# Attention, MoE and RMS-norm MoE in one kernel: low-weight transfers and half of the first v go to ScalarE's DMA queue, and the opening order changes

## The chip, the core and the metric

The kernel runs on one core of one Trainium2 chip. The metric is the device time of one execution in microseconds, as the median of several runs. TensorE does the matrix multiplications, VectorE, ScalarE and GpSimd the elementwise work, and SyncE issues DMA transfers. ScalarE can issue DMAs too, in its own instruction stream: such an instruction waits there for the buffer or the data that it needs, and what stands behind it on ScalarE waits with it.

## The reference

Three stages follow one another on 4608 tokens of width 512.

```python
def _attn_ref(q, k, v):          # (8, 8, 576, 64), in chunks of 64 tokens
    scores = scale * np.matmul(q_c, k_c.transpose(0, 1, 2, 4, 3))
    attn = np.exp(scores - np.max(scores, axis=-1, keepdims=True))
    attn = attn / (np.sum(attn, axis=-1, keepdims=True) + 1e-09)
    return np.matmul(attn, v_c)

def _moe_ref(x, w_gate, w_val, w_out):   # 512 -> 1536 -> 512
    g = x @ w_gate
    return (g * (1.0 / (1.0 + np.exp(-g))) * (x @ w_val)) @ w_out

def _moe2_ref(x, w_gate, w_val, w_out, rms_g):
    xn = x / np.sqrt(np.mean(x * x, axis=-1, keepdims=True) + 1e-06) * rms_g
    # then the same as _moe_ref, on xn
```

The result of the attention, laid out by tokens, is the x of the first MoE, and its result the x of the second. The weights arrive as 64-bit floating point numbers; q, k and v as 32-bit ones.

## The kernel before, in words

**Precision.** Each operand of a large product is kept as a high part, rounded to TensorE's fast 32-bit format, and a low part, the rest. A product is then three matmuls, high by high, high by low and low by high (mm3, lines 476 to 479).

**First MoE.** The tokens are cut into 9 blocks of 512 (index j), the hidden width into 12 tiles of 128 (index f). One iteration (j, f), of 108 in all, does emit_g (12 matmuls, then a tanh on ScalarE and a product on VectorE, line 490), emit_v (12 matmuls, then a product on VectorE, line 506, and a rounding of the hidden tile on ScalarE, line 509), and emit_y of the iteration before (12 matmuls into four PSUM banks that collect over f). The gate and the value have one PSUM bank each, so the next gate tile waits for line 490, the next value tile for line 506.

**Weights.** There are 36 weight tiles: g, v and o for each f. In block 0, the "head", they are loaded raw (pre_w1, line 979, through load_w64, line 101) and converted one by one. `conv1(z)` (line 995) works on tile z: `rebase` of tile z+1 (two passes on ScalarE, lines 112 and 116, the tiles cr and cm), `to_f32` of tile z (two passes on VectorE, lines 131 and 134, of which the second reads the first's result, and a rounding on ScalarE to the high part, line 144), `to_lo` of tile z-1 (a subtraction on VectorE, line 152, to the low part), and the next raw load. High parts stay in SBUF. Low parts do not fit: each is written to a scratch in DRAM (lo1_d, called lo_scratch in the trace) and read again in each of the blocks 1 to 8. Three buffers each hold low g and low v tiles, four low o tiles. In the head a new low tile needs a buffer whose write has landed and whose matmuls are done.

The writes are kept in a list, `keep`, and issued on SyncE when more than five are waiting (line 1006). `load_lo` (line 157) fetches the three low tiles of an iteration two iterations ahead, on SyncE as well, 96 times three loads; the first is called in the head, at f = 10.

**Attention.** It runs in tiles of 128 tokens. For the first four tiles it stands ahead of the first MoE and is written out by hand (lines 1026 to 1060): trans_tok transposes q and k on TensorE and copies them on ScalarE; att_s makes the scores; att_m subtracts the maximum (VectorE) and takes the exponential (ScalarE); att_n sums and inverts (VectorE) and scales (GpSimd); att_t transposes the probabilities on TensorE and copies them on ScalarE (line 408); att_pv multiplies by v and rounds to the high x (ScalarE, line 453); att_lo subtracts for the low x (VectorE, line 471). The later tiles are laid into the positions of the iterations, three to an iteration, by `put` and `spread`; `run(p)` calls what stands at a position. `spread` issues a list of loads on SyncE in equal parts over a number of positions.

**Order.** Every engine works through its own instructions in the order in which the program writes them. SyncE has nearly all DMAs: q and k of tiles 0 to 3 (load_tok, two each), v of the first eight chunks (load_v(0), 16 pieces of 64 KB) with the first raw weights between, later loads of q, k and v, the raw weights, the writes of low weights and the loads of them.

**After the first MoE.** The second MoE uses combinations of weight blocks and other loops (from line 1134); its weights come through load_ring on SyncE. The change does not touch it.

Of the kernel before, what the change touches and what calls it, by code (L numbers as in the profile page):

```python
# [9 lines left out]
F32 = mybir.dt.float32  # L10
# [9 lines left out]
def tile_kernel(  # L20
# [17 lines left out]
    nc = tc.nc  # L38
# [66 lines left out]
    keep = []  # L105
# [3 lines left out]
    def rebase(l, nm, f):  # L109
        high = stage[l, nm, f][:, :, 1]  # L110
        r = cv.tile([P, KD * P], U32, tag="cr", bufs=3, name=f"cr{nm}{f}_{l}")
        nc.scalar.activation(r.bitcast(F32), high.bitcast(F32), AF.Copy, scale=2.0 ** -112)
        m = None
        if l == 0:
            m = cv.tile([P, KD * P], U32, tag="cm", bufs=2, name=f"cm{nm}{f}_{l}")
            nc.scalar.activation(
                m, stage[l, nm, f][:, :, 0], AF.Copy,
                scale=2.0 ** -29 * (1.0 - 2.0 ** -16), bias=7.5 * 2.0 ** -16 - 0.5,
            )
        half[l, nm, f] = (r, m)  # L120

    def to_f32(l, nm, f):
        t = stage.pop((l, nm, f))
        low, high = t[:, :, 0], t[:, :, 1]
        r, m = half.pop((l, nm, f))
        if m is None:
            m = cv.tile([P, KD * P], U32, tag="cm", bufs=1, name=f"cm{nm}{f}_{l}")
            nc.vector.tensor_scalar(
                out=m, in0=low, scalar1=29, scalar2=None, op0=ALU.logical_shift_right
            )  # L130
        nc.vector.scalar_tensor_tensor(
            out=m, in0=high, scalar=0x80000000, in1=m, op0=ALU.bitwise_and, op1=ALU.bitwise_or
        )
        nc.vector.scalar_tensor_tensor(
            out=r, in0=r, scalar=3, in1=m, op0=ALU.logical_shift_left, op1=ALU.bitwise_or
        )
        r = r.bitcast(F32)
        if l == 0:
            hi = wraw.tile([P, KD * P], F32R, tag=f"w{nm}{f}", name=f"w{nm}{f}_0")
            whi[0, nm, f] = hi  # L140
        else:
            flat[nm, f] = r
            return
        nc.scalar.copy(hi, r)
        made[l, nm, f] = (r, hi)
# [11 lines left out]
    def load_lo(l, j, f):  # L157
        for z, nm in enumerate("gvo"):
            t = wlo.tile([P, KD * P], F32R, tag=f"l{nm}", bufs=LB[nm], name=f"l{nm}_{l}_{j}_{f}")
            nc.sync.dma_start(out=t.bitcast(F32), in_=lo1_d[z, f])  # L160
            wl_[l, j, f, nm] = t

    flat = {}
# [145 lines left out]
    def issue(dmas):  # L309
        for o, i in dmas:  # L310
            nc.sync.dma_start(out=o, in_=i)  # L311
# [332 lines left out]
    for x, (l, j) in enumerate(seq):  # L644
# [32 lines left out]
        if x > 0 and seq[x - 1][0] == 0:  # L677
# [8 lines left out]
            for d in range(KD):  # L686
                put(l, j, 28 + 2 * d, lambda pj=pj, d=d: rms_x(pj, d))

    w2 = [(nm, f) for fp in range(NP2) for nm in "gvo" for f in (fp, fp + NP2)]
    slots = [(j, 3 * f) for j in range(1, NB - 1) for f in range(0, NF, 2)]  # L690
    for (nm, f), (j, pos) in zip(w2, slots):
# [280 lines left out]
    with tc.manual_schedule():  # L972
# [22 lines left out]
        def conv1(z):  # L995
            if z < 0 or z > len(w1) + 2:
                return
            if z + 1 < len(w1):
                rebase(0, *w1[z + 1])
            if z < len(w1):  # L1000
                to_f32(0, *w1[z])
            if 0 < z <= len(w1):
                if z > 1:
                    to_lo(*w1[z - 1])
                pre_w1(z + 6 if z < 6 else 12 if z < 8 else z + 5)
            while len(keep) > (5 if z < len(w1) else 0):
                nc.sync.dma_start(out=keep[0][0], in_=keep[0][1])
                keep.pop(0)

        NI = NW // P  # L1010
# [2 lines left out]
        issue(load_tok(2))  # L1013
        issue(load_tok(3))
        first_v = load_v(0)
        issue(first_v[:len(first_v) // 2])
        pre_w1(1)
        issue(first_v[len(first_v) // 2:])
        pre_w1(3)
        issue(load_tok(4))  # L1020
        pre_w1(7)
        nc.sync.dma_start(out=rg, in_=moe2_rms_g.rearrange("(c p) -> p c", p=P))
        later = load_v(1)
        sb_ = ("a", "yb")
        xb_ = (("g", "v"), ("y0", "y1"))
        trans_tok(0, xb_[0])
        trans_tok(1, xb_[1])
        att_s(0, sb_[0])
        att_m(0)
        trans_tok(2, xb_[0])  # L1030
        att_s(1, sb_[1])
        att_m(1)
        trans_tok(3, xb_[1])
        att_n(0)
        att_s(2, sb_[0])
        att_m(2)
        att_n(1)
        att_s(3, sb_[1])
        rebase(0, *w1[0])
        att_m(3)  # L1040
        att_n(2)
        att_t(0, xb_[0][0])
        att_t(1, xb_[1][0])
        to_f32(0, *w1[0])
        att_n(3)
        att_pv(0, 0, "a")
        att_pv(1, 0, "yb")
        att_lo(0, 0)
# [3 lines left out]
        att_lo(1, 0)  # L1052
        att_pv(2, 0, "a")
        att_pv(3, 0, "yb")
        att_lo(2, 0)
        att_lo(3, 0)
        rebase(0, *w1[1])
        conv1(1)
        conv1(2)
        conv1(3)  # L1060
# [6 lines left out]
        for n, (l, j, f) in enumerate(iters):  # L1067
            def run(p):
                for fn in at.get(3 * n + p, ()):
                    fn()  # L1070

            head = (l, j) == (0, 0)
            if (j, f) == (1, 0):
                conv.close()
                cv = open_pool(conv, "cv2", 2, "right")
            if (j, f) == (NB - 1, 0):
                conv.close()
                attn.close()
                X2 = open_pool(two, "x2", 1, "right")
                x_load(0, 0)  # L1080
                xops = x_prep(0, 0)
            if (j, f) == (NB - 1, 8):
                load_ring(4)

            if head and f == 0:
                issue(later + load_tok(5))
            if head and f in (1, 2):
                issue(load_tok(5 + f))
                if f == 1:
                    issue(load_v(2))  # L1090
            if n + 2 < len(iters) and n + 2 >= NF:
                load_lo(*iters[n + 2])
            if (j, f) == (NB - 1, 8):
                x_load(0, 1)
            if (j, f) == (NB - 1, 9):
                load_ring(16)
                xops = xops + x_prep(0, 1)
            if prev is not None:
                lo()
            sg, product = emit_g(l, j, f)  # L1100
            run(0)
            if head:
                conv1(3 * f + 4)
            v_product, lo = emit_v(l, j, f, sg)
            product()
            run(1)
            if head:
                conv1(3 * f + 5)
            if prev is not None:
                emit_y(*prev)  # L1110
            v_product()
            if prev is not None and prev[2] == NF - 1:
                evac_y(*prev[:2])
            run(2)
            if head:
                conv1(3 * f + 6)
            if j == NB - 1 and f >= 2:
                for _ in range(4 if f > 6 else 2):
                    if xops:
                        xops.pop(0)()  # L1120
            prev = (l, j, f)
# [115 lines left out]
```

## Time and profile before

| | |
|---|---|
| median of 3 runs | 1772.9 us (1772.55 to 1774.66) |
| profiled execution | 1774.16 us, span of the trace 1772.4 us |
| TensorE busy | 1738.1 us, 98% of the span |
| VectorE busy | 1267.1 us, 71% |
| ScalarE busy | 673.0 us, 38% |
| GpSimd busy | 394.9 us, 22% |
| SyncE's DMA queue | 377.68 MB, 72.8% of the 16 engines' span |
| ScalarE's DMA queue | 0.20 MB, 0.1% |
| mean granted TensorE clock | 0.996 |

In the profile PE is TensorE, DVE is VectorE, ACT is ScalarE, POOL is GpSimd; SPq and ACTq are the DMA issues of SyncE and ScalarE. A timeline row is the start, the duration, the engine, the source line, the operation with output and input, and the count; a bracket at its end gives the engine's idle time before it and what ended that. Consecutive instructions of one kind are merged into one row. The ends of matmuls are modelled, so matmul rows overlap. The granted clock is a share of the full 2.4 GHz; 0.50 is the lower level of 1.2 GHz. The DMA share is the mean busy share of the 16 DMA engines, which can come out a little over one.

### The profile page before, as it was taken

What the parts mean: (1) busy time and instruction counts of PE and PEld (TensorE: products, weight loads), DVE (VectorE), ACT (ScalarE), POOL (GpSimd) and SP (SyncE); (2) the same over time, 40 slices, a digit from 0 to 9 for tenths busy, and PEclk for the clock granted to TensorE, in tenths of its full rate; (3) what the DMA queues carried; (4) which work ended last, traced back from release to release, by engine and by line L of the source; (5) the groups of instructions that cost most, each with busy time, mean ns of one, the idle gap of its engine ahead of it and who ended that gap; (6) DMA issues with size and microseconds to landing.
All of it is one profiled execution on the core that took longest, in us unless ns stands there. A gap on an engine that the chain in (4) does not pass through costs nothing.

```text
span 1772.4 us, 28903 instructions
## 1 busy us (share of the span) xinstructions
PE 1738.1 (98%) x10086; PEld 1469.6 (83%) x10086; DVE 1267.1 (71%) x2250; ACT 673.0 (38%) x1248; POOL 394.9 (22%) x391
## 2 busy tenths in 40 slices
PE   6998999999999999999999999999999999999998
PEld 5787778888888888888888888888888888999998
DVE  6896687887878888786635566954794478568566
ACT  6672323323332332332123334623453254344343
POOL 1001325343342534233031200200120011002000
PEclk8999999999999999999999999999999999999999
DMA  9996777776687867864336477787678768987986
GB/s 220 292 252 176 217 205 216 217 228 206 183 245 216 228 187 223 222 201 137 123 115 200 140 238 195 197 261 218 192 213 246 212 184 234 293 269 227 312 254 176
DMA packets 451457, 379.73 MB, mean 214 GB/s; under 512 B 275696, under 2 KB 302320, under 8 KB 451312
## 3 DMA queue, kind: packets, MB, share of 16 engines
q1 hardware_dynamic: 449712, 377.68, 72.8%
q8 instruction: 81, 1.33, 0.3%
q14 instruction: 64, 0.52, 0.1%
q10 hardware_dynamic: 1600, 0.20, 0.1%
HBM read 316.41 MB, written 61.34 MB: 213 GB/s over the span
## 4 chain that ended last, share of the span: by engine, by line
PE 86%; DVE 6%; DMA 3%; SPq 2%; ACT 1%; issue 1%; POOL 0%; ACTq 0%; DVEq 0%; POOLq 0%
PE v L477 5%; PE g L479 5%; PE v L479 5%; PE v L478 5%; PE g L477 5%; PE g L478 5%; PE y L477 3%; PE y L478 2%; PE y L479 2%; PE y_b L479 2%; PE y_b L478 2%; PE y_b L477 2%; SPq L311 2%; DVE pT L393 1%; PE ygA L477 1%
## 5 line engine op out<-in xcount | busy, mean ns | idle before, releaser
L477 PE MATMUL v<-xh,wv 128*128 128x512 f32 x432 | 170.0, 394 | 8.2 <-DVE sg L506 8.2
L477 PE MATMUL g<-xh,wg 128*128 128x512 f32 x432 | 169.8, 393 | 2.1 <-DVE sg L490 1.4
L479 PE MATMUL g<-xh,lg 128*128 128x512 f32 x432 | 169.1, 392 | 1.9 <-DMA lg<-lo_scratch 1.9
L509 ACT CAST hh<-sg 128x512 fp32r<-128x512 f32 x108 | 67.1, 622 | 269.9 <-DVE sg L506 269.8
L478 PE MATMUL g<-xl,wg 128*128 128x512 f32 x432 | 169.1, 391 | 0.3 <-DVE xl L471 0.3
L478 PE MATMUL v<-xl,wv 128*128 128x512 f32 x432 | 168.3, 390 | 0.0
L479 PE MATMUL v<-xh,lv 128*128 128x512 f32 x432 | 168.3, 390 | 0.0
L873 POOL TENSOR_TENSOR h<-h,h 128x512 f32<-128x512 f32 (+1 forms) x30 | 37.1, 1235 | 521.2 <-DVE h L851 521.2
L393 DVE STREAM_TRANSPOSE pT<-p 32x128 f32<-32x128 f32 x448 | 135.5, 302 | 7.2 <-POOL p L377 0.9
L490 DVE SCALAR_TENSOR_TENSOR sg<-sg,g 128x512 f32<-128x512 f32 x108 | 73.0, 676 | 87.0 <-ACT sg L489 86.6
L489 ACT ACTIVATE sg<-g 128x512 f32<-128x512 f32 x108 | 64.4, 596 | 184.0 <-PE g L479 183.2
L909 DVE TENSOR_TENSOR hl<-h,hh 128x512 fp32r<-128x512 f32 (+1 forms) x180 | 121.6, 705 | 6.0 <-ACT hh L908 5.9
L908 ACT CAST hh<-h 128x512 fp32r<-128x512 f32 (+1 forms) x180 | 100.3, 577 | 47.2 <-PE yvA L479 20.4
L832 DVE TENSOR_TENSOR sgt<-sgt,sig 128x512 f32<-128x512 f32 (+1 forms) x90 | 58.3, 648 | 74.1 <-ACT sig L831 74.0
L831 ACT ACTIVATE sig<-sgt 128x512 f32<-128x512 f32 (+1 forms) x90 | 53.1, 590 | 147.1 <-DVE sgt L839 147.1
L511 DVE TENSOR_TENSOR hl<-sg,hh 128x512 fp32r<-128x512 f32 x108 | 86.6, 802 | 29.0 <-ACT hh L509 28.9
L377 POOL TENSOR_TENSOR p<-p,r 128x512 f32<-128x512 f32 x36 | 38.9, 1081 | 297.7 <-DVE r L376 270.9
L477 PEld LDWEIGHTS v<-xh,wv 128*128 128x128 f32 x432 | 81.3, 188 | 28.5 <-DVE sg L506 6.5
L477 PEld LDWEIGHTS g<-xh,wg 128*128 128x128 f32 x432 | 81.4, 188 | 20.2 <-DVE sg L490 2.3
L479 PEld LDWEIGHTS g<-xh,lg 128*128 128x128 f32 x432 | 81.5, 189 | 19.3 <-DMA lg<-lo_scratch 2.3
L506 DVE SCALAR_TENSOR_TENSOR sg<-v,sg 128x512 f32<-128x512 f32 x108 | 74.0, 685 | 32.7 <-PE v L479 31.3
L478 PEld LDWEIGHTS g<-xl,wg 128*128 128x128 f32 x432 | 81.4, 188 | 17.6 <-DVE xl L471 0.6
(806 smaller groups left out, 4703.7 us busy)
## 6 DMA issues: line engine op xcount, KB each, us to landing
wrg<-w_scratch SPq DMA_DIRECT2D x210, 256.0 KB, 3.4
wrv<-w_scratch SPq DMA_DIRECT2D x210, 256.0 KB, 3.4
wro<-w_scratch SPq DMA_DIRECT2D x210, 256.0 KB, 3.1
lg<-lo_scratch SPq DMA_DIRECT2D x96, 256.0 KB, 2.9
lv<-lo_scratch SPq DMA_DIRECT2D x96, 256.0 KB, 3.3
lo<-lo_scratch SPq DMA_DIRECT2D x96, 256.0 KB, 3.8
w_scratch<-wsg SPq DMA_DIRECT2D x42, 256.0 KB, 2.8
w_scratch<-wsv SPq DMA_DIRECT2D x42, 256.0 KB, 2.7
```

Of the source, the lines that this page charges most:

```text
L393: nc.vector.transpose(out=pT[o:o + 32, :, r:r + 32], in_=pt[r:r + 32, :, z, b * 32:b * 32 + 32])
L477: nc.tensor.matmul(o, sh, mh, start=first, stop=False, skip_group_check=free)
L478: nc.tensor.matmul(o, sh, ml, start=False, stop=False, skip_group_check=free)
L479: nc.tensor.matmul(o, sl, mh, start=False, stop=last, skip_group_check=free)
L489: nc.scalar.activation(sg[:, :n], g[:, :n], AF.Tanh, scale=0.5)
L490: return sg, lambda: nc.vector.scalar_tensor_tensor(out=sg[:, :n], in0=sg[:, :n], scalar=1.0, in1=g[:, :n], op0=ALU.add, op1=ALU.mult)
L506: nc.vector.scalar_tensor_tensor(out=sg[:, :n], in0=vv[:, :n], scalar=0.5, in1=sg[:, :n], op0=ALU.mult, op1=ALU.mult)
L509: nc.scalar.copy(hh[:, :n], sg[:, :n])
L511: return product, lambda: nc.vector.tensor_sub(hl[:, :n], sg[:, :n], hh[:, :n].bitcast(F32))
L832: nc.vector.tensor_mul(t[:, :tw], src[:, :tw], sg[:, :tw])
L908: nc.scalar.copy(hh[:, :tw], src)
L909: nc.vector.tensor_sub(hl[:, :tw], src, hh[:, :tw].bitcast(F32))
```

## The change

Seven edits:

- `load_lo` issues its loads from ScalarE in place of SyncE.
- `to_f32` takes a function, `between`, that it calls between the two passes on VectorE; conv1 hands it the `to_lo` of the tile before, which so far came after both passes.
- The writes of low weights: up to tile 23 as before; from there at most two are kept in place of five, and they are issued from ScalarE.
- Of the 16 pieces of the first v, SyncE issues the first four, then the first raw weight, then four more; ScalarE issues the other eight in four pairs (`more_v`), written into the code behind trans_tok(1), trans_tok(2), trans_tok(3) and att_m(2).
- The first conversion: rebase of the first weight stands behind att_m(3) and att_n(2); the transpose att_t(0) stands ahead of att_m(3); att_n(3) stands ahead of to_f32 of the first weight.
- The rebase of the second weight stands two att_lo earlier.
- The ten loads of load_v(2), so far issued together in iteration f = 1, are spread one each over the positions 2 to 11 of block 0.

```diff
-    def to_f32(l, nm, f):
+    def to_f32(l, nm, f, between=None):
...
             out=m, in0=high, scalar=0x80000000, in1=m, op0=ALU.bitwise_and, op1=ALU.bitwise_or
         )
+        if between is not None:
+            between()
         nc.vector.scalar_tensor_tensor(
...
-            nc.sync.dma_start(out=t.bitcast(F32), in_=lo1_d[z, f])
+            nc.scalar.dma_start(out=t.bitcast(F32), in_=lo1_d[z, f])
...
+    spread(0, 0, 2, 10, lambda: load_v(2))
...
+            low = (lambda: to_lo(*w1[z - 1])) if 1 < z <= len(w1) else None
             if z < len(w1):
-                to_f32(0, *w1[z])
+                to_f32(0, *w1[z], between=low)
+            elif low is not None:
+                low()
             if 0 < z <= len(w1):
-                if z > 1:
-                    to_lo(*w1[z - 1])
                 pre_w1(z + 6 if z < 6 else 12 if z < 8 else z + 5)
-            while len(keep) > (5 if z < len(w1) else 0):
-                nc.sync.dma_start(out=keep[0][0], in_=keep[0][1])
+            while len(keep) > (5 if z < 24 else 2 if z < len(w1) else 0):
+                queue = nc.sync if z < 24 else nc.scalar
+                queue.dma_start(out=keep[0][0], in_=keep[0][1])
                 keep.pop(0)
...
         first_v = load_v(0)
-        issue(first_v[:len(first_v) // 2])
+        half_v = len(first_v) // 2
+        issue(first_v[:half_v // 2])
         pre_w1(1)
-        issue(first_v[len(first_v) // 2:])
+        issue(first_v[half_v // 2:half_v])
         pre_w1(3)
...
+        def more_v(n):
+            for o, i in first_v[half_v + n * half_v // 4:half_v + (n + 1) * half_v // 4]:
+                nc.scalar.dma_start(out=o, in_=i)
+
...
         trans_tok(1, xb_[1])
+        more_v(0)
         att_s(0, sb_[0])
         att_m(0)
         trans_tok(2, xb_[0])
+        more_v(1)
         att_s(1, sb_[1])
         att_m(1)
         trans_tok(3, xb_[1])
+        more_v(2)
         att_n(0)
         att_s(2, sb_[0])
         att_m(2)
+        more_v(3)
         att_n(1)
         att_s(3, sb_[1])
-        rebase(0, *w1[0])
+        att_t(0, xb_[0][0])
         att_m(3)
         att_n(2)
-        att_t(0, xb_[0][0])
+        rebase(0, *w1[0])
         att_t(1, xb_[1][0])
+        att_n(3)
         to_f32(0, *w1[0])
-        att_n(3)
...
+        rebase(0, *w1[1])
         att_lo(2, 0)
         att_lo(3, 0)
-        rebase(0, *w1[1])
...
-                if f == 1:
-                    issue(load_v(2))
```

## Rows read from the trace of the kernel before

**Rows 1.** Windows: stretch, us, busy of PE PEld DVE ACT POOL, PEclk, DMA share, GB/s

```profile
60.00:80.00 20.00, 18.60 (x114) 14.68 (x113) 17.10 (x29) 14.99 (x27) 0.15 (x1) 1.00 1.05 345
...
100.00:120.00 20.00, 20.00 (x120) 16.25 (x119) 19.69 (x34) 15.03 (x27) 1.30 (x1) 1.00 0.93 270
```

**Rows 2.** Page, the span in 40 equal slices, TensorE's busy tenths

```profile
PE   6998999999999999999999999999999999999998
```

**Rows 3.** Timeline of TensorE, 0 to 62 us

```profile
22.98 1.99 PE L435 MATMUL xb<-pT,xv 64*64 64x64 f32 x64 [3.93 <-ACT pT L408]
...
28.98 0.50 PE L477 MATMUL g<-xh,wg 128*128 128x512 f32 x1 [0.73 <-ACT xh L453]
...
37.69 0.69 PE L339 MATMUL s<-kT,qT 64*64 64x64 f32 x32 [1.44 <-ACT kT L305]
```

**Rows 4.** Timeline of TensorE, 60 to 150 us

```profile
62.68 0.66 PE L296 MATMUL qkP<-ident,tq 128*128 128x128 f32 x4 [0.94 <-DVE xl L471]
...
78.72 0.50 PE L477 MATMUL g<-xh,wg 128*128 128x512 f32 x1 [0.46 <-DVE sg L490]
...
83.07 0.47 PE L477 MATMUL v<-xh,wv 128*128 128x512 f32 x1 [0.88 <-DVE sg L506]
...
141.54 0.47 PE L477 MATMUL v<-xh,wv 128*128 128x512 f32 x1 [2.87 <-DVE sg L506]
```

**Rows 5.** Timeline of TensorE, 174 to 182 us

```profile
177.11 0.50 PE L479 MATMUL g<-xh,lg 128*128 128x512 f32 x1 [1.89 <-DMA lg<-lo_scratch]
```

**Rows 6.** Windows of TensorE alone: stretch, us, PE busy, PEclk, DMA share, GB/s

```profile
176.00:178.00 2.00, 0.89 (x3) 0.92 0.98 327
178.00:180.00 2.00, 2.00 (x6) 0.50 0.71 117
180.00:182.00 2.00, 2.00 (x8) 0.73 0.41 67
```

**Rows 7.** Timeline of ScalarE, 0 to 62 us

```profile
11.41 0.63 ACT L365 ACTIVATE p<-p 128x512 f32<-128x512 f32 x1 [1.96 <-DVE p L359]
...
20.73 0.66 ACT L112 ACTIVATE crg<-w64g 128x512 f32<-128x512 f32 x1 [4.46 <-DMA w64g<-in_moe_w_gate_dram]
...
22.36 1.05 ACT L408 COPY pT<-tp 128x512 f32<-128x512 f32 x2
```

**Rows 8.** Timeline of SyncE's DMA issues, 0 to 80 us

```profile
8.55 6.76 SPq L311 DMA_DIRECT2D xv<-in_v_dram  x8
...
16.00 5.31 SPq L311 DMA_DIRECT2D xv<-in_v_dram  x8
...
45.78 9.32 SPq L311 DMA_DIRECT2D xv<-in_v_dram  x10
55.15 0.60 SPq L1007 DMA_DIRECT2D lo_scratch<-lv  x1
```

**Rows 9.** Timeline of VectorE, 28 to 135 us

```profile
38.81 0.69 DVE L131 SCALAR_TENSOR_TENSOR cmo<-stage,cmo 128x512 uint32<-128x512 uint32 x1 [0.17 <-ACT cmo L116]
39.53 0.69 DVE L134 SCALAR_TENSOR_TENSOR cro<-cro,cmo 128x512 uint32<-128x512 uint32 x1
40.14 0.68 DVE L152 TENSOR_TENSOR lv<-crv,wv 128x512 fp32r<-128x512 f32 x1
...
60.73 0.69 DVE L152 TENSOR_TENSOR lv<-crv,wv 128x512 fp32r<-128x512 f32 x1 [2.28 <-DMA lo_scratch<-lv]
...
133.68 0.69 DVE L152 TENSOR_TENSOR lg<-crg,wg 128x512 fp32r<-128x512 f32 x1 [2.57 <-DMA lo_scratch<-lg]
```

**Rows 10.** Timeline of SyncE's DMA issues, 158 to 175 us

```profile
171.31 2.96 SPq L311 DMA_DIRECT2D xq<-in_q_dram  x4
174.31 0.45 SPq L160 DMA_DIRECT2D lg<-lo_scratch  x1
```

**Rows 11.** Page, costliest groups: busy, mean ns of one, idle before, releaser

```profile
L489 ACT ACTIVATE sg<-g 128x512 f32<-128x512 f32 x108 | 64.4, 596 | 184.0 <-PE g L479 183.2
```

**Rows 12.** Line 160, its DMA issues: ns min/median/max, first and last start us

```profile
L160 SPq DMA_DIRECT2D lo<-lo_scratch x96: 319/382/1299, 132.8 to 958.6; - x96
```

## The prediction

> **What bounds the kernel now.** I read the stretches of 20 us first, then TensorE's timeline for its gaps, then the timelines of whatever ended each gap. [rows 1] shows two things. From 100 to 120 us TensorE is busy for all 20.00 us while VectorE has 19.69, so the first token block is a near tie of these two. From 60 to 80 us TensorE lacks 1.40 us, and the DMA share is 1.05, so the transfers are a third candidate there. The slices of the whole span [rows 2] have TensorE at nine tenths or more from the fifth slice, 177 us, to the last but one. So what can be won lies in the first 180 us, in three places.
>
> The start: TensorE waits 3.93 us for the first P·V product, and the first gate matmul begins at 28.98 us [rows 3]. The first block: four waits of 1.44 [rows 3], 0.94, 0.46 and 0.88 us [rows 4], 3.7 us together, all but the first ended by VectorE. Its end: TensorE stands 2.87 us before the matmul at 141.54 us [rows 4], and 1.89 us at 177.11 us for a low weight block that had not landed [rows 5]. After this last gap the granted clock falls to 0.50 [rows 6], the lower of the two levels. Lost clock times stretch is 2 x 0.08 + 2 x 0.50 + 2 x 0.27 = 1.7 us.
>
> **The change, part by part.** The profiled execution took 1774.16 us, 1.3 us over the median of 1772.9. I make the sum against 1774.16 and carry it to the median at the end.
>
> *Start (half of the first v, first conversion moved).* ScalarE idles 4.46 us for the first raw weight tile, does its two passes, and only then copies the first transposed probabilities (at 22.36 us) for which TensorE waits [rows 7]. The order written in the code puts rebase ahead of them, so a weight not yet needed holds the attention up. SyncE reaches that weight at 8.55 + 6.76 = 15.3 us because eight v pieces stand before it; eight more follow, 5.31 us [rows 8]. Now four stand before it, so the weight goes out some 3.4 us earlier, the next two weights, with eight pieces fewer in front, some 5 to 6 us earlier, and the passes stand behind all four exponentials. In exchange ScalarE issues eight pieces in four pairs. No row shows such an issue on ScalarE; SyncE's 0.66 to 0.85 us each (5.31/8 and 6.76/8) bound it at 5.3 to 6.8 us. ScalarE's idle time there is 1.96 + 4.46 = 6.4 us [rows 7]. What is queued behind each pair is the next exponential or copy, and behind those VectorE's sums, GpSimd's scaling and TensorE's transposes. At the lower price 1.1 us of idle time is left, and the two passes, about 1.1 us, leave the path of the first copy. That is 2.2 us, less something for the exponential behind the second pair, which comes late: I take -1.5 us. Ends: -3.9 (the whole wait goes) and +2.3 (issues at 0.85 that each hold something up, and more of it if both queues slow each other). I am near the lower price because the second eight, without the first loads ahead of them, cost that.
>
> *The subtraction between the two VectorE passes.* In [rows 9] the pass at 39.53 starts 0.72 us after the one at 38.81 whose result it reads; the subtraction at 40.14 starts 0.61 us behind an operation it does not read. Putting the subtraction in between gives 0.11 us for each of 35 tiles, 3.9 us of VectorE over the first block. The Trainium skill (VectorE: DVE Perf Modes, The DRAIN you can't avoid) says that the next operation starts only when the pipe has emptied, whatever the dependence. By that rule the reorder would give nothing and the sum would end some 1 us higher; the trace disagrees, 0.72 against 0.61. The cost: a subtraction that waits for a free low buffer now holds back the second pass and ScalarE's rounding as well. That happened at 60.73 us, for 2.28 us, and at 133.68 us, for 2.57 us [rows 9].
>
> *The third v spread.* SyncE spends 9.32 us on ten v pieces from 45.78 us, and the low-weight write behind them goes out only at 55.15 us [rows 8]; the subtraction at 60.73 us waits for that write. Spread one to a position, each piece puts at most about 0.93 us in front of what follows, so that stall should go, and with it the 0.94 us of TensorE at 62.68 us. The tile is needed only at position 16 of the block, and the last piece goes out at position 11: nothing late.
>
> For the first block the two items and the earlier weights give at most the 3.7 us and at least nothing (VectorE still behind, or transfers the limit). I take -2.0: VectorE regains 3.9 us plus the 2.28 us stall by 87 us, but TensorE also arrives earlier, so the first wait (1.44 us, ScalarE's conversions before a copy of attention) largely stays.
>
> *Late low-weight writes.* From the 25th conversion they are held back by two instead of five and go out on ScalarE: 18 of 36. The stall at 133.68 us is one of them, behind attention loads on SyncE, and the wait at 141.54 us is its follow-on through the product on VectorE. With three conversions more of lead both go: -2.87 us, ends 0 and -2.87. The 18 issues, at about 0.4 us, are 7 us of ScalarE, which is 15.03 of 20 us busy [rows 1]. TensorE has the longer work there, which covers them; if VectorE's queue turns late, ScalarE's issues add to it.
>
> *Low-weight loads.* 288 loads leave SyncE, where one went out at 174.31 us behind attention pieces, the last four of which took 2.96 us [rows 10]: the direct cause of the 1.89 us. -1.89 and -1.7 for the clock, ends 0 and -3.6. On ScalarE each group of three stands after the rounding of the last hidden tile and before the next tanh; the third load waits until the output matmuls of two iterations before are done. Queued behind it are the tanh, VectorE's gate product, and with it the next use of the gate's PSUM bank. ScalarE idles 184.0/108 = 1.70 us before a tanh, for TensorE [rows 11], and three issues at the median of 0.38 us are 1.15 us [rows 12]. So I cost them at nothing, hidden in that idle time; the bounds are nothing and, at the slowest issue of 1.30 us [rows 12], 2.2 us over the idle time of an iteration.
>
> Moving the second conversion ahead of two subtractions changes no engine's own order: nothing.
>
> Sum: 1774.2 - 1.5 - 2.0 - 2.9 - 1.9 - 1.7 = 1764.2 us, which at the median is 1762.9 us. The best ends give 1774.2 - 3.9 - 3.7 - 2.9 - 3.6 = 1760.1, at the median 1758.8 us.
>
> **The rivals.**
> Only the late stalls go. The first block stays with VectorE or with the transfers, and a shorter start merely waits longer there: 1774.2 - 2.9 - 3.6 - 1.3 = 1766.4 us. For it: DMA share 1.05 and 19.69 of 20 us of VectorE [rows 1]. Against it: the measured stalls behind SyncE's issues.
>
> The transfers are the limit, so another queue changes nothing and the stalls move: about 1771 us, of which 1.9 or less is won. The DMA share of 1.05 [rows 1] speaks for it. Against it, a 64 KB piece takes 0.66 us of SyncE's time, and the loads stand in line while SyncE issues. The Trainium skill (DMA: Bandwidth & Descriptors, Issuing engines are not separate DMA queues) says that all queues share the same engines and that a second one saves only issue time. The trace agrees in part: issue time is just what SyncE lacks at 16 and at 174 us [rows 8, 10].
>
> ScalarE is held by the loads. In 20.00 us 120 matmuls run [rows 1], so the 24 of value and output that follow a gate tile take 24 x 0.17 = 4.0 us; tanh and product take 0.6 each of that, so 2.8 us are to spare before the gate's bank is wanted again. This case decides once three issues outlast 1.70 + 2.8 us, that is at 1.5 us an issue. If 0.2 us then reaches TensorE in each of 96 iterations, that is +19: 1762.9 + 19.2 = 1782.1 us. Against it: the median of 0.38 us [rows 12]. For it: no row shows ScalarE issuing beside its arithmetic.
>
> That the change does not do what it says: all eight pieces, the 18 writes and the ten spread pieces are still issued, once each; only the second conversion's move is empty.
>
> **How the numbers follow.** Forecast 0.60 at 1762.9 us (own range 1758.8 to 1766), only the late stalls 0.17, transfers 0.14, ScalarE held 0.09. 0.2%, about what a measurement of this kernel tells from no change, is 3.5 us. The first two are faster, 0.77; the third same, 0.14; the last slower, 0.09. The range goes from the best ends, 1758, to 1770, which takes in the second case and the edge of the third.
>
> **What would show it.** The first gate matmul near 27.5 us; no waits ended by a low-weight write on VectorE; no gap of TensorE near 133 to 140 us and none for lg; the clock at full in the stretches that answer to 176 to 182 us; VectorE's second pass 0.6 us behind the subtraction; ScalarE's waits before tanh shorter while TensorE's after 200 us stay. The prediction is wrong if the first gate matmul begins after 29 us, if TensorE gains waits for the gate product between 200 and 950 us, or if the 3.7 us return as waits on ScalarE.

## The result, and the profile after

The kernel after took 1782.53 us in the median of six runs (1781.39 to 1784.45), beside 1773.51 (1772.03 to 1775.78) for six runs of the kernel before: ratio 1.0052, 95% interval [1.0039, 1.0064]. The change made the kernel slower by 9 us, where 1762.9 us were forecast. The profiled execution took 1781.53 us with a span of 1779.7 us, 7.3 us over the span of before.

Both kernels run the same 10086 matmuls in the same order. So one subtracts the start of each matmul in the trace of before from that of the same matmul in the trace of after, and sees where time is won and lost. Start before, start after, difference, all in us:

```
 22.98   21.43  -1.55   first P·V product
 28.98   29.74  +0.76   first gate matmul
 31.32   33.19  +1.87   eighth gate matmul
 83.07   80.49  -2.58   value product
141.54  135.59  -5.95   value product
144.47  141.16  -3.32   P·V product
179.80  173.72  -6.09   gate product
182.24  179.50  -2.74   value product
200.36  203.04  +2.69   value product
322.23  326.03  +3.80   value product
357.64  362.89  +5.25   value product
377.29  383.69  +6.40   scores
1766.35 1773.99 +7.65   last matmul
```

The first three rows rest on one execution each and say little. Run 2 below opens as before does, and in its trace the same matmuls start 1.50 and 0.47 us earlier and 0.64 us later than in before's; in the eight traces that open as after does, the eighth gate matmul lies between 0.40 us earlier and 2.17 us later. From 83 us on the rows are well beyond that.

At 135 us and again at 173 us the kernel after is 6 us ahead. From the second point to the end it loses 13.7 us. The losses begin at waits of TensorE, here in its timeline from 125 to 204 us:

```profile
135.59 0.47 PE L479 MATMUL v<-xh,wv 128*128 128x512 f32 x1
...
141.16 0.69 PE L437 MATMUL xb<-pT,xv 64*64 64x64 f32 x32 [2.58 <-ACT pT L410]
...
177.21 0.79 PE L479 MATMUL v<-xh,wv 128*128 128x512 f32 x1 [2.65 <-DVE sg L508]
...
199.70 0.69 PE L341 MATMUL both<-kT,qT 64*64 64x64 f32 x32 [3.76 <-DVE kT L324]
```

The wait of 2.87 us before the product that was at 141.54 us [rows 4] is gone, and so is the wait for lg [rows 5]. Three new waits follow. The granted clock falls behind the last two of them, as it did before behind the wait for lg [rows 6] (windows, with the columns of [rows 1]):

```profile
60.00:80.00 20.00, 20.00 (x122) 16.41 (x121) 18.73 (x32) 14.46 (x27) 1.33 (x1) 1.00 1.01 328
100.00:120.00 20.00, 20.00 (x124) 16.44 (x123) 18.47 (x31) 16.07 (x30) 1.04 (x1) 1.00 0.87 269
...
178.00:180.00 2.00, 2.00 (x6) 1.52 (x6) 1.81 (x4) 0.63 (x1) 0.00 (x0) 0.50 0.46 91
...
202.00:204.00 2.00, 2.00 (x6) 1.52 (x6) 1.14 (x2) 1.20 (x3) 1.92 (x4) 0.50 0.84 190
```

The first two rows answer to [rows 1]: the first block is now full on TensorE, with VectorE at 18.73 and 18.47 us. It did what was wanted of it.

**What ends the new waits.** Followed back from 177.21 us, first on VectorE, whose product sg ended TensorE's wait:

```profile
174.60 0.43 DVE L128 TENSOR_SCALAR cmg<-w64g 128x512 uint32<-128x512 uint32 x1 [6.86 <-DMA w64g<-in_moe_w_gate_dram]
...
176.47 0.68 DVE L508 SCALAR_TENSOR_TENSOR sg<-v,sg 128x512 f32<-128x512 f32 x1
```

The product stood behind the conversion of a raw weight that landed late. SyncE's issues say why it was late:

```profile
159.34 1.92 SPq L313 DMA_DIRECT2D xv<-in_v_dram  x3
167.31 2.67 SPq L313 DMA_DIRECT2D xq<-in_q_dram  x4
170.03 0.97 SPq L101 DMA_DIRECT2D w64g<-in_moe_w_gate_dram  x1
```

SyncE issued nothing from 161.26 to 167.31 us, and the raw weight went out at 170.03 us, where before it went at 164.10. ScalarE's timeline has the other half:

```profile
164.61 0.62 ACT L511 CAST hh<-sg 128x512 fp32r<-128x512 f32 x1 [7.01 <-DVE sg L508]
164.67 0.33 ACTq L162 DMA_DIRECT2D lg<-lo_scratch  x1
...
174.60 0.67 ACT L112 ACTIVATE crg<-w64g 128x512 f32<-128x512 f32 x1 [7.93 <-DMA w64g<-in_moe_w_gate_dram]
```

The low-weight load could go out only behind the rounding of the hidden tile, which had waited 7.01 us for VectorE. And SyncE, about to fetch rows of q that have nothing to do with lg, waited for that load to land. The list of waits names it outright (us in total, times, longest), first SyncE's queue, then ScalarE:

```profile
SPq L313 <- DMA lg<-lo_scratch: 53.7, 27, 6.0
```

```profile
ACT sg L491 <- DMA lg<-lo_scratch: 21.0, 9, 3.4
ACT sg L491 <- DMA lo<-lo_scratch: 20.6, 5, 4.6
ACT wsv L190 <- DMA w_scratch<-wsv: 17.6, 10, 7.1
ACT crg L112 <- DMA w64g<-in_moe_w_gate_dram: 16.4, 3, 8.0
ACT wso L190 <- DMA w_scratch<-wso: 12.6, 9, 2.7
```

The two lines of sg (the tanh) say less than they seem to. The list puts a wait for several things down to the one that came last, and a tanh behind load instructions also waits for its own gate tile. In 12 of these 14 waits, 35.5 of the 41.6 us, the tanh starts more than 0.5 us after the last load was issued, and right behind the last matmul of its gate. Here is one, on ScalarE and then on TensorE:

```profile
866.51 0.33 ACTq L162 DMA_DIRECT2D lo<-lo_scratch  x1
869.29 0.60 ACT L491 ACTIVATE sg<-g 128x512 f32<-128x512 f32 x1 [4.15 <-DMA lo<-lo_scratch]
```

```profile
868.81 0.39 PE L481 MATMUL g<-xh,lg 128*128 128x512 f32 x1
```

The load was out at 866.84 us, the gate was done at 869.20: it is TensorE that this tanh waited for. The other three lines are waits for what the instruction itself needs. Line 112 needs the raw weight that SyncE fetched late. Line 190 rounds weights of the second MoE into four buffers, and a buffer is free again only when SyncE has written it to DRAM; these waits come to 36.4 us (17.6, 12.6 and 6.2 for wsg) against 8.7 us in before. So a SyncE that is held holds ScalarE in turn, and with it the loads behind.

Of the other two waits of TensorE, the one at 199.70 us has the same form: VectorE had waited 6.76 us for the raw weight that SyncE issued at 191.52 us; why it went out only then isn't followed here. At 141.16 us ScalarE's copy of probabilities stood behind the loads of lv and lo, which went out at 137.33 and 139.60 us, once ScalarE's own writes of 134.43 and 134.83 us had landed.

**Why an issue of q waits for lg.** The program as built marks the end of each DMA of SyncE and ScalarE on one of eight semaphores, dealt in turn in the order of the program, whichever engine issues it. Before a semaphore is used again, its last DMA must have landed. So every DMA waits for the eighth one before it. The trace of after shows it: eight semaphores serve all DMAs of both engines, and the load of lg at 164.67 us and the piece of q at 167.31 us signal the same one. While one engine issues nearly everything in that order, this costs little. With two issuers, each is held wherever the other is behind. The DMA instructions of the built programs that wait for one of the other issuer (the last two kernels are from the experiments):

```
                          SyncE for ScalarE's   ScalarE for SyncE's
before                              0                    1
after                             159                  109
after, loads on SyncE              18                   21
the same with dummies             125                  231
```

### The profile page after: what moved, and what is told of

It is laid out like the page before. It is cut to its first block, busy times and chain, and to the rows that moved or that the text cites. A ratio compares the mean times of both kernels' runs of the same rounds, so it can differ in the third digit from the quotient of the medians.

```text
span 1779.7 us, 28752 instructions
## 1 busy us (share of the span) xinstructions
PE 1741.8 (98%) x10086; PEld 1472.0 (83%) x10086; DVE 1263.4 (71%) x2250; ACT 676.2 (38%) x1248; POOL 394.7 (22%) x391
## 4 chain that ended last, share of the span: by engine, by line
PE 80%; DVE 8%; DMA 6%; issue 2%; ACT 2%; SPq 1%; POOL 1%; ACTq 0%; DVEq 0%; POOLq 0%
PE v L479 4%; PE v L481 4%; PE v L480 4%; PE g L479 4%; PE g L481 4%; PE g L480 4%; PE y L479 2%; PE y L480 2%; PE y L481 2%; PE y_b L481 2%; PE y_b L479 2%; PE y_b L480 2%; PE ygA L479 1%; PE ygA L480 1%; PE ygA L481 1%
## 5 line engine op out<-in xcount | busy, mean ns | idle before, releaser
L491 ACT ACTIVATE sg<-g 128x512 f32<-128x512 f32 x108 | 64.7, 599 | 190.2 <-PE g L481 119.5
L513 DVE TENSOR_TENSOR hl<-sg,hh 128x512 fp32r<-128x512 f32 x108 | 86.3, 799 | 29.2 <-ACT hh L511 29.1
L481 PEld LDWEIGHTS v<-xh,lv 128*128 128x128 f32 x432 | 81.7, 189 | 17.5
```

The source lines that it names most:

```text
L481: nc.tensor.matmul(o, sl, mh, start=False, stop=last, skip_group_check=free)
L491: nc.scalar.activation(sg[:, :n], g[:, :n], AF.Tanh, scale=0.5)
L513: return product, lambda: nc.vector.tensor_sub(hl[:, :n], sg[:, :n], hh[:, :n].bitcast(F32))
```

## The experiments

Three theories at the outset. Coupled (L in the expectations): the loads on ScalarE tie the two queues together through the eight semaphores. Held (H): the loads merely stand ahead of the tanh and hold ScalarE's arithmetic. Start (S): the new opening or the writes cost the time, and the loads are innocent. Lines are those of after, except where told.

**1. The loads back on SyncE, the rest as after.**

```diff
-            nc.scalar.dma_start(out=t.bitcast(F32), in_=lo1_d[z, f])
+            nc.sync.dma_start(out=t.bitcast(F32), in_=lo1_d[z, f])
```

> The changed kernel with one edit undone: the low-weight loads go out on SyncE again; all the rest of the change stays. Theory L (shared completion semaphores: each DMA waits for the eighth one before it in program order, on whichever queue that one is, so loads held back on ScalarE hold back SyncE's transfers, and the other way round) and theory H (ScalarE itself is held by its loads, so that tanh and conversions come late) both put the loss on the loads: about 1767 us (1764 to 1770), with the 6 us by which TensorE was ahead at 141 and 180 us kept to the end. Theory S (the start, the late writes or the spread third v cost the time): 1777 us or more.

1768.29 us (before in the same set 1773.44), ratio 0.9972 [0.9962, 0.9983]. The other six edits together win 5 us; the loads turn that into a loss of 9. The start theory falls. What is left is the old wait for lg, with its half clock (TensorE's timeline, then a window):

```profile
172.38 0.50 PE L481 MATMUL g<-xh,lg 128*128 128x512 f32 x1 [2.26 <-DMA lg<-lo_scratch]
```

```profile
174.00:176.00 2.00, 2.00 (x6) 1.60 (x5) 0.00 (x0) 0.00 (x0) 1.33 (x2) 0.50 0.42 69
```

**2. Only the loads moved, the rest as before** (the edit above reversed, in the kernel before; its lines).

> The kernel before with one edit alone: the low-weight loads go out on ScalarE. L and H: slower than before by about what the first run gives back, 1783 to 1790 us, with SyncE waiting for lg, lv and lo to land and the raw weight w64g late on ScalarE. S: 1770 to 1774 us, since the wait of 1.89 us for lg goes and nothing comes in its place.

1783.76 us, 1.0057 [1.0042, 1.0072]: 10.3 us lost by this edit alone. SyncE's queue waits for ScalarE's loads, and ScalarE for SyncE's writes of the second MoE's weights (39.3 us with wso and wsg, 8.7 in before):

```profile
SPq L311 <- DMA lg<-lo_scratch: 49.0, 28, 6.4
```

```profile
ACT wsv L188 <- DMA w_scratch<-wsv: 18.4, 9, 7.1
```

**3. The loads on GpSimd**, whose DMAs have semaphores of their own in the built program.

```diff
+            nc.gpsimd.dma_start(out=t.bitcast(F32), in_=lo1_d[z, f])
```

> The changed kernel with the low-weight loads issued by GpSimd, whose DMAs complete on semaphores of their own, so neither SyncE nor ScalarE waits for them. L: most of the loss goes, 1765 to 1772 us, unless GpSimd, held by the loads' own waits, brings the attention's scaling too late (then waits of TensorE or VectorE on GpSimd's p show it). H: the same as L, since ScalarE has no loads. S: stays at 1782 us.

1795.67 us, 1.0118 [1.01, 1.0135]: slower still, a miss for the expectation. The waits of SyncE and ScalarE for low weights did go, and TensorE has no waits between 150 and 210 us. Another cost came in their place. VectorE at 378.74 us and GpSimd beside it:

```profile
378.74 3.33 DVE L513 TENSOR_TENSOR hl<-sg,hh 128x512 fp32r<-128x512 f32 x1
```

```profile
377.45 0.56 POOL L162 DMA_DIRECT2D lg<-lo_scratch  x1
378.00 0.54 POOL L162 DMA_DIRECT2D lv<-lo_scratch  x1
378.54 0.54 POOL L162 DMA_DIRECT2D lo<-lo_scratch  x1
```

```profile
PE both L341 <- DVE kT L324: 12.6, 5, 5.0
```

An issue takes GpSimd 0.54 us, and a VectorE subtraction that overlaps the last of them took 3.33 us; the mean of L513 is 982 ns here, 799 ns in after, and VectorE's busy time 1307.9 us against 1263.4. What makes it slow isn't shown. The run tells nothing of the price of the coupling, since it swaps one cost for another.

**4. The loads on ScalarE, but behind the tanh**, which parts the theories coupled and held.

```diff
-            if n + 2 < len(iters) and n + 2 >= NF:
-                load_lo(*iters[n + 2])
...
             sg, product = emit_g(l, j, f)
+            if n + 2 < len(iters) and n + 2 >= NF:
+                load_lo(*iters[n + 2])
```

> The changed kernel with the loads still on ScalarE, but written behind the tanh of the iteration instead of ahead of it: the matmuls that they wait for are done by then, so ScalarE does not stand for a buffer. H: the loss goes, about 1767 us, and no wait of tanh on a low-weight DMA is left. L: SyncE still waits for the loads in 155 places and they go out later than before, so 1780 us or more, with SyncE's waits for lg, lv and lo as long as in the changed kernel or longer.

1785.54 us, 1.007 [1.0053, 1.0087]. No tanh stands directly behind these loads any more, and the kernel is no faster. SyncE's queue and ScalarE:

```profile
SPq L313 <- DMA lg<-lo_scratch: 68.0, 33, 4.3
```

```profile
ACT crg L112 <- DMA w64g<-in_moe_w_gate_dram: 18.7, 2, 10.8
```

SyncE waits more than in after (53.7 us), raw weights still come late, and no wait of a tanh is put down to a DMA any more. The theory that the place ahead of the tanh decides falls.

**5. Loads on SyncE as in 1, and ScalarE issues three dummies in their old place**: 512 bytes each, into a tile that nobody reads (lines two further on). They have no data and no buffer in common with other work, and 288 of them move 0.15 MB.

```diff
+                for _ in range(3):
+                    c = idled[0] % 24
+                    nc.scalar.dma_start(out=idle[:, c:c + 1], in_=moe2_rms_g[0:P].rearrange("(c p) -> p c", p=P))
+                    idled[0] += 1
```

> The first run's kernel (low-weight loads on SyncE) with three extra transfers of 512 bytes issued on ScalarE at each place where the changed kernel issued its three loads; nothing reads them, they wait for no buffer and for no matmul. L: they still take their turns at the eight shared semaphores, so SyncE's transfers wait behind ScalarE and ScalarE behind SyncE's: 1776 us or more, with tanh waiting on xq, xv or w64g and SyncE waiting on the extra transfers. H, in the form that the loads' own waits for buffers hold ScalarE: nothing lost, 1767 to 1770 us. H, in the form that the issue time of ScalarE costs: the same as the changed kernel's loads, but then tanh starts late without a wait on a transfer.

1842.08 us, 1.0383 [1.0368, 1.0399]: 74 us over run 1. SyncE's queue, then ScalarE:

```profile
SPq L315 <- DMA idle<-in_moe_rms_g_dram: 45.5, 30, 6.3
SPq L164 <- DMA idle<-in_moe_rms_g_dram: 42.2, 25, 5.3
```

```profile
ACT wsv L192 <- DMA w_scratch<-wsv: 34.9, 12, 7.3
```

SyncE's loads of q, k, v (L315) and of low weights (L164) wait for transfers that nobody reads. Besides the DMA engines, the shared semaphores are all that the built program gives them in common, and on the engines the dummies weigh little: their 41,474 packets raise ScalarE's queue from 1.0% (run 1) to 2.0% of the engines' span. Nor is it the issue, 0.44 us in the median. That the semaphores make SyncE wait for ScalarE is shown by this. The way back goes largely through buffers: ScalarE's rounding of the second MoE's weights (line 192 here) waits 92.7 us for SyncE's writes, 34.9 of them in the line above, against 7.3 us in run 1. How far each added wait carries to TensorE, and why dummies cost five times what the loads did, wasn't taken apart further; nor does any run part the loads' 14 us into waits for semaphores and for buffers.

**6. Run 1 with the first v all on SyncE** (`more_v` removed, two eights as before; the other opening edits stay).

> The first run's kernel with all 16 pieces of the first v on SyncE again (eight, the first raw weight, eight), the moved first conversion kept. If the fourth pair on ScalarE waited there for the first raw weight to land (same shared semaphores), the first P.V product now starts near 19.5 us, the gate matmuls near 28 us and the time falls by 1 to 2 us to about 1766.5 us. If ScalarE's copies were late for another reason, or the second eight now land late, no change: 1768 to 1769 us.

1768.74 us, 0.9976 [0.9965, 0.9987]: no difference from run 1 that these intervals can tell. The first P·V product starts at 19.53 us, as the first case had it, 1.0 us earlier than in run 1 (20.55, and 21.43 in after with the same opening), and at 144 us TensorE is 3.1 us behind run 1.

**7. Run 1 with the late writes on SyncE, five kept back, as before.**

```diff
-            while len(keep) > (5 if z < 24 else 2 if z < len(w1) else 0):
-                queue = nc.sync if z < 24 else nc.scalar
+            while len(keep) > (5 if z < len(w1) else 0):
+                queue = nc.sync
```

> The first run's kernel with the late low-weight writes as before (on SyncE, five held back). If these writes were the cause of the 2.87 us at 141 us, the wait comes back: 1770 to 1772 us, and VectorE's subtraction waits for a write again. If the spread and the earlier conversions alone had removed it: 1768 us.

1770.63 us, 0.9986 [0.9976, 0.9997]. VectorE waits 4.3 and 3.2 us for a write again, and TensorE 3.3 us before the product that had the 2.87 us. TensorE is 5.1 us behind run 1 at the product that starts run 1's at 135.43 us, 3.2 at the wait for lg and 1.4 at the end. The writes win 5 us locally, of which most is then spent waiting elsewhere.

**8. Run 1 with the third v issued in one go.**

> The first run's kernel with the third v issued in one go again. If the spread removed the stall of 2.28 us on VectorE at 61 us, it comes back, and TensorE loses the 1 to 3 us that it had gained by 83 us: 1769 to 1771 us. If VectorE's shorter conversion alone had gained them: 1768 us.

1769.37 us, 0.9978 [0.9968, 0.9987]: TensorE is 1.1 us later than in run 1 at 81 us, 1.5 us at 83 us and 0.03 us later at the end. No difference there. VectorE's stall of 2.28 us at 61 us does not come back, so the spread isn't needed to remove it.

**9. Run 1 with the loads one iteration earlier**, behind the output product and ahead of the value product, against the wait for lg.

```diff
-            if n + 2 < len(iters) and n + 2 >= NF:
-                load_lo(*iters[n + 2])
...
                 emit_y(*prev)
+            if NF <= n + 3 < len(iters):
+                load_lo(*iters[n + 3])
```

> The first run's kernel (low-weight loads on SyncE) with each group of three loads written one step earlier, behind the output matmuls and ahead of the attention loads of the last position of an iteration. If the 1.89 us of before, 2.3 us in the first run, came only from the attention pieces that stood ahead of the loads in SyncE's queue, that wait and the half-clock stretch behind it go: 1763 to 1765 us, with no wait of TensorE for lg. If SyncE had no time there in any order, the wait moves to the attention's q and k: 1767 to 1769 us.

1771.27 us, 0.9989 [0.998, 0.9998], above both cases of the expectation. The wait for lg went, and another came at 143 us (ScalarE, then TensorE):

```profile
141.58 0.38 ACTq L1013 DMA_DIRECT2D lo_scratch<-lo  x1
142.06 0.60 ACT L491 ACTIVATE sg<-g 128x512 f32<-128x512 f32 x1 [8.32 <-DMA xk<-in_k_dram]
```

```profile
143.18 1.13 PE L437 MATMUL xb<-pT,xv 64*64 64x64 f32 x32 [4.86 <-ACT pT L410]
```

ScalarE's last write waited until a piece of k that SyncE issued had landed, and the tanh and the copy of probabilities behind it waited with it: the coupling again, from the other side.

**10. Run 9 without `between`** (the subtraction after both passes).

> The kernel of the run above with the subtraction back behind the two VectorE passes. If the 0.11 us for each of 35 tiles counts, VectorE is 3.9 us busier in the first block and TensorE is later by 1 to 3 us there: 1765 to 1767 us. If VectorE has slack by now, no difference from the run above.

1771.72 us, 0.9991 [0.9982, 1.0]: 0.45 us over run 9, inside both intervals. TensorE is no later in the first block either.

**11. Run 9 with the first v all on SyncE.**

> The kernel of the first of these three with the first v on SyncE again. If the 1.7 us by which the opening was earlier in that form last, 1762 to 1764 us; if the first block gives them back at its end as before (its last attention tile waited for a copy), the same as the first of the three.

1773.12 us, 0.9998 [0.9988, 1.0007]: nothing won; the intervals of this and of run 9 overlap.

**12. Run 1 with the loads early only from the second group of block 1 on, and the last writes of low weights on SyncE.**

```diff
-                queue = nc.sync if z < 24 else nc.scalar
+                queue = nc.scalar if 24 <= z < len(w1) else nc.sync
...
-            if n + 2 < len(iters) and n + 2 >= NF:
+            if NF <= n + 2 <= NF + 2:
                 load_lo(*iters[n + 2])
...
+            if NF <= n and n + 3 < len(iters):
+                load_lo(*iters[n + 3])
```

> The kernel of the first experiment (ScalarE issues the late low writes and half of the first v, SyncE the low-weight loads) with two edits: from the second group on the low weights are loaded right behind the combine, ahead of the V product (the wait on lg at 172 us was left over in the first experiment), and the last writes of the low weights go on SyncE, since ScalarE's last one was held at 141 us when the loads came early. If what remains is only those waits (the theory that the order of issue over both queues decides): the 2.3 us at 172 us and the half clock behind it go, ScalarE's wait at the end of the head goes too, some 3 to 5 us below the first experiment: 1764 us (1762 to 1767). If SyncE has no spare time in any order (the rival): what is gained at 172 us comes back as waits on raw weights or rows of x, 1767 to 1771 us.

1767.41 us (before 1772.25), 0.9969 [0.9959, 0.9979]. In the trace the wait of 2.26 us shrinks to two of 0.46 and 1.28 us, the clock at 174 us stays at full, and ScalarE's wait at the head's end reaches TensorE with 0.54 us (TensorE's timeline, then a window of TensorE alone):

```profile
170.18 0.50 PE L481 MATMUL g<-xh,lg 128*128 128x512 f32 x1 [0.46 <-DMA lg<-lo_scratch]
...
179.95 0.50 PE L481 MATMUL g<-xh,lg 128*128 128x512 f32 x1 [1.28 <-DMA lg<-lo_scratch]
```

```profile
174.00:176.00 2.00, 2.00 (x10) 1.00 0.42 68
```

The span of this profile is 1764.8 us, 2.4 us below that of run 1. The medians don't follow: 0.9969 and 0.9972 can't be told apart. So 1764 us is not reached, the measured time lies in the rival's range of 1767 to 1771 us, and whether the last 2 us of the trace are really won stays open. It beats both kernels by its interval; so does run 1.

## Why the prediction was wrong

**The step that failed** is the sentence on the loads: "So I cost them at nothing, hidden in that idle time". The issue price was right: 0.33 to 0.39 us in the median, three of them 1.1 us, in idle time of 1.7 us. But an issue isn't all that a load brings to an engine. It waits there, and on this program it waits for the eighth DMA before it too. The prediction counted what is queued behind a load on ScalarE and what its buffer waits for. It didn't ask what SyncE's next DMA waits for once a load of ScalarE is one of the eight before it. Instead of -1.9 - 1.7 + 0, the edit costs 10.3 us alone (run 2) and 14.2 us beside the others (1782.53 - 1768.29).

The part that it gained came as forecast: no wait for lg and TensorE 6.1 us ahead at 173.72 us. Without the loads the terms of the prediction are -1.5 - 2.0 - 2.9 = -6.4 us; run 1 measured -5.15. So the rest of the sum came close, but that is luck: the start missed one way and the first block the other. Of its own signs of being wrong, the first came (a first gate matmul after 29 us). The second didn't: what TensorE waits for more between 200 and 960 us is the value product (6.1 us against 3.6), not the gate's. Term by term:

**Start, forecast -1.5: +1.9 in the trace of after.** TensorE in after:

```profile
21.43 1.13 PE L437 MATMUL xb<-pT,xv 64*64 64x64 f32 x32 [1.78 <-ACT pT L410]
...
29.74 0.50 PE L479 MATMUL g<-xh,wg 128*128 128x512 f32 x1 [0.69 <-ACT xh L455]
```

The first P·V product came 1.55 us earlier, which run 2 does with the old opening too (21.48 us); the eight traces that open as after does have it 1.55 to 4.27 us earlier. The first gate matmul was to come near 27.5 us and came at 29.74 against 28.98 [rows 3]. ScalarE's rows show an issue that took three times its price, and a last pair that went out only at 19.44 us:

```profile
15.06 1.95 ACTq L1034 DMA_DIRECT2D xv<-in_v_dram  x1
...
19.44 1.31 ACTq L1034 DMA_DIRECT2D xv<-in_v_dram  x2
20.79 0.59 ACT L410 COPY pT<-tp 128x512 f32<-128x512 f32 x1 [3.10 <-issue]
```

The price of one was 0.63 us in the median of eight, just under the lower end of 0.66. But in the built program the last pair waits for the semaphore of the raw weight that SyncE issued at 12.72 us. So the weight not yet needed, moved off the path of the copies by hand, still held them through the semaphores. SyncE was held as well: the first weight went out 2.6 us earlier than before (forecast 3.4), the next two 1.8 and 1.9 us earlier at 19.61 and 20.13 us (forecast 5 to 6), the second weight behind ScalarE's piece of 13.05 us on the same semaphore. Then TensorE's clock, at 1.00 in 30 to 34 us before, was 0.55 and 0.60:

```profile
30.00:32.00 2.00, 1.78 (x5) 0.55 1.06 381
32.00:34.00 2.00, 2.00 (x7) 0.60 1.13 306
```

The clock isn't the new opening's doing, though, for with the old one run 2 has it low too:

```profile
30.00:32.00 2.00, 2.00 (x7) 0.50 1.10 348
```

With the eighth gate matmul 1.4 to 2.2 us later than in before in seven of the eight traces, and 0.64 us later in run 2, the start is rather later by about 1 us than earlier. That lies inside the end of +2.3 given for this term; the gain did not come. In runs 6 and 11, which take back its v pieces, the end of the kernel doesn't move beyond the intervals.

**First block, forecast -2.0: measured -4.5** (+1.87 at 31 us to -2.58 at 83 us). It is past the stated end of -3.7. That end left out waits of before in the same block, these two among them:

```profile
47.86 0.51 PE L477 MATMUL g<-xh,wg 128*128 128x512 f32 x1 [0.58 <-DVE sg L490]
...
52.21 0.47 PE L477 MATMUL v<-xh,wv 128*128 128x512 f32 x1 [0.85 <-DVE sg L506]
```

None of the four waits of [rows 3, 4] is left in after; of 0.35, 0.90 and 0.34 us between 48 and 56 us, the first two stand where the two above stood. The start and this term together were forecast at -3.5 and came to -2.6. The gain over this stretch is 4.4 to 4.5 us in all eight traces that open as after does. Run 2, with the old block, is 1.4 us quicker there than before's trace too, so some 3 us of it are left for the change. Run 8, without the spread, gains 3.2 us in the stretch, and run 10, without the subtraction between the passes, 4.9: the spread helps here, the new order of the passes doesn't. (The prediction also had all 3.9 us of VectorE regained by 87 us, where 35 tiles take the whole block.) On VectorE itself the subtraction between the passes does what was said:

```profile
126.60 0.68 DVE L131 SCALAR_TENSOR_TENSOR cmv<-w64v,cmv 128x512 uint32<-128x512 uint32 x1
127.20 0.69 DVE L154 TENSOR_TENSOR lg<-crg,wg 128x512 fp32r<-128x512 f32 x1
127.80 0.68 DVE L136 SCALAR_TENSOR_TENSOR crv<-crv,cmv 128x512 uint32<-128x512 uint32 x1
```

All are 0.60 us apart, where the dependent pair of [rows 9] was 0.72 apart. The operations take 0.68 to 0.69 us, so each starts before the one ahead has ended. That goes against the rule of the Trainium skill (VectorE: DVE Perf Modes, The DRAIN you can't avoid) as the prediction read it. But the same paragraph adds that "A next op that is not held starts earlier", which the prediction left out, so the rows don't contradict the page. Runs 8 and 10 show no difference at the end for this or for the spread third v.

**Late writes, forecast -2.87: measured -3.4** (-2.58 to -5.95). Right in place and size in the trace; 2.3 us between the medians of runs 1 and 7, whose intervals overlap.

**The rivals.** "ScalarE is held by the loads" gave 1782.1 us. The time agrees, the mechanism doesn't: its condition was an issue of 1.5 us, the issues take 0.4, and run 4, which moves the tanh ahead of the loads, is as slow. (The bound of the loads' term took 1.30 us for the slowest issue, which [rows 12] gives for lo alone; lv's slowest in before is 1.58.) Its place was wrong too: no 0.2 us in each of 96 iterations, but a few waits of 0.5 to 4 us, some with lost clock behind them, which are the steps of the table at 141, 177, 199, 326, 363 and 384 us. ScalarE's wait before the tanh was to shrink; the page of after has it at 190.2 us against 184.0 [rows 11] and puts 119.5 of it down to TensorE. Of the other 70.7 us some 40 are waits for the gate as well, as at 869.29 us, so at most about 30 come from the loads:

```profile
L491 ACT ACTIVATE sg<-g 128x512 f32<-128x512 f32 x108 | 64.7, 599 | 190.2 <-PE g L481 119.5
```

"Transfers are the limit" fails too: run 1 moves the same bytes and is faster than before. The Trainium skill (DMA: Bandwidth & Descriptors, Issuing engines are not separate DMA queues) says that a second issuer saves issue time only. Run 5 goes beyond that rule: here a second issuer can cost 74 us with 0.15 MB.

## What to carry to other kernels

Before a DMA is moved to a second engine, look at which completion semaphore it gets and which DMA must land before that semaphore is free: where the semaphores are dealt in program order over all queues, an in-order engine that also computes will hold the other queue whenever its arithmetic is late. A sign of it in the list of waits is a load that waits for the landing of a tile it has no business with. On an engine that computes, check such a line against the end of the instruction's own input before believing it. When a move is costed, the price of the issue is the small part; ask what each queue's next transfer waits for.

## What the runs showed of the hardware that wasn't expected

GpSimd's issue of a 256 KB load takes 0.54 us of its time, against 0.33 to 0.39 us on ScalarE, and a VectorE operation beside a group of three took 3.33 us in place of about 0.7 (run 3).

The clock doesn't answer to a wait's length alone. It was 0.50 behind waits of 2.26 us (run 1), 2.65 and 3.76 us (after). But behind after's wait of 2.58 us at 141.16 us it stayed at full, and so it did in before behind the 2.87 us at 141.54 us (1.00 from 142 to 144 us there too; window of TensorE in after):

```profile
142.00:144.00 2.00, 2.00 (x10) 1.00 0.57 110
```

What else decides it, these runs don't show.
